# A three-stage kernel (clustered attention, dense MLP, mixture of experts): the order of work on ScalarE and GpSimd among the expert tiles, and of one subtraction at the start

## The chip, the cores and the metric

The kernel runs on one core of one Trainium2 chip. The metric is the device time of one execution in microseconds (us). Every time beyond the table of runs comes from one execution that the hardware profiler recorded. The engines are named as the profile names them: PE (TensorE's matmuls), PEld (its weight loads), DVE (VectorE), ACT (ScalarE), POOL (GpSimd) and SP (SyncE, which only starts DMAs here).

## What is computed

Three functions follow one another, all in float32:

```python
q_assign = argmax(q_n @ c_n.T)                 # nearest of 16 centroids, per head
mask = q_assign[..., :, None] == k_assign[..., None, :]
scores = where(mask, scale * q @ k.T, -1e9)
attn = softmax(scores) @ v                     # 2 batches, 8 heads, 768 tokens, 64
x = attn.reshape(1536, 512)
h = x @ w_in
x = (h * sigmoid(h)) @ w_out                   # 512 -> 2048 -> 512
logits = x @ w_gate + modality_bias[modality_id]
e_idx = argmax(logits)                         # 8 experts
gate_w = softmax(logits)[e_idx]
out = gate_w * (relu(x @ w1[e_idx]) @ w2[e_idx])   # 512 -> 1024 -> 512
```

## The kernel before

Products in float32 are made of three matmuls each: every operand is split into a high part (a copy rounded for PE) and a low part (the operand minus its high part). The helper at L200 subtracts, those at L202 and L209 copy (on ACT, and on POOL or DVE). So every weight and every activation is converted by two instructions on two engines before PE can use it.

**Attention** works through eight head pairs. For a pair, the loads of q, k and v come in on SP; q is scaled (L404, POOL, for every pair but the first); q and k are transposed (L422 is one of the ways, on DVE), split into high and low parts (for the low part of the first pair's k: two subtractions L200 on POOL, into `opn_0KX`) and moved to other partitions by DMAs on SP (L489). The cluster of each token is found by `c0` to `c5` (L503 to L523: transposes and reductions on DVE, one matmul L519 on PE). PE then does scores (L594 and L597), transposes of the probabilities (L633) and the product with v (L699). The reciprocals of the sums go to a buffer in memory (L686, `rsc<-rr`) and come back spread over partitions (L691, `rb<-rsc`) for the scaling on DVE at L704. At the start PE runs matmuls on a constant (L304) whose results nobody reads.

**The dense MLP** lies between 231 and about 520 us; the change doesn't touch its code.

**The experts.** After the routing the tokens of each expert stand in rows of an index table. Twelve tiles of 128 tokens (0 to 11) follow one another, and four small slots for what is left over (`SMALL_AT` names the tiles behind which they stand; `small` is the function). For one tile `slot` issues:

- the gather of its rows from `x2d` by an indirect DMA on POOL (L1403), each row with 512 numbers and, behind them, its 8 gate logits;
- four transposes on PE (L1408), the copy to high on ACT (L1412) and the low part on DVE (L1415);
- the first product, 24 matmuls (L1429), into two banks of 512;
- for each of the two banks the ReLU on ACT (L1444), four transposes on PE (L1449), a copy on ACT (L1454) and a subtraction on DVE (L1457);
- the second product, 24 matmuls (L1471);
- the exponential of the gate logits with its sum on ACT (L1481), three short operations on DVE (L1484 to L1488) that make 1/sum;
- the output scaling on ACT (L1495) and the scatter to the output, an indirect DMA on POOL (L1498).

A small slot has the same steps with 64 or 32 rows (gather L1537, first product L1560, ReLU L1567, transposes L1572, copy L1576, second product L1589, exponential L1596, output L1606, scatter L1609). The weights of an expert come in eight chunks on SP (L1360 and L1363; a load is skipped at run time where the next tile has the same expert), and each chunk is split by L202 on ACT and L200 on DVE.

**What sets the order.** The instructions of each engine stand in a fixed order in the program. It is found when the kernel is built: every piece of work is given to `op` with an estimated duration, the pieces that it depends on, the buffers it uses and a priority, and `Sched.run` plays the engines forward, taking on each engine the ready piece with the smallest `prio`. The tables `cp` (tiles) and `cs` (small slots) hold offsets to the priorities of the kinds of pieces (`tx` for the gathered rows' transposes and, before, the exponential; `rl` for the ReLU; `ga` for gathers), and `gl` and `late` are the planner's figures for how long a gather takes. A dependency in these lists shapes the order only; on the chip an instruction waits for the data and buffers that it uses. An engine does its instructions strictly in order, so one that waits holds all behind it.

The exponential of a tile was placed by these two calls:

```python
oe = op("Act", 1480 if t == 0 else 195, fe, deps=[og, M1[4]], uses=[gb, eb], alloc=[eb], prio=tx)
o = orel = op("Act", 480, fr, deps=[o_m, orel], uses=[hs_, hbs[x]], alloc=[] if x else [hs_], prio=pr + cp["rl"])
```

Of the kernel before, what the change touches and what calls it, by code (L numbers as in the profile page):

```python
# [228 lines left out]
def attention(tc, sc, pools, q, k, v, centroids, ident, xT, opts):  # L229
    nc = tc.nc  # L230
    if True:
# [14 lines left out]
        op = sc.op  # L246
# [45 lines left out]
        o = op("DVE", 400, cnorm1, deps=[o_cl], prio=-90)  # L292
        o = op("Act", 100, lambda: nc.scalar.activation(cn, css, AF.Sqrt), deps=[o], prio=-90)
        o = o_norm = op("DVE", 1900, cnorm2, deps=[o], prio=-90)
# [19 lines left out]
        o = op("PE", 213, ctr, deps=[o, o_id], uses=[mbc], alloc=[mbc], prio=-90)  # L314
# [20 lines left out]
        raws, ops, Sops, xops, wait, held = {}, {}, {}, {}, [], {}  # L335
# [39 lines left out]
        def prep(p):  # L375
# [156 lines left out]
            o = scores  # L532
            cl = []
            steps = [dve(c0), dve(c1), dve(c2), dve(c3), [("PE", 163, c4)], dve(c5)]
            for n, a in enumerate(steps):
                o = op(a, 0, None, deps=[o], uses=[cb] + ([mb] if n in (0, 4, 5) else []), alloc=[cb] if n == 0 else [],
                       prio=base + (5 + 0.1 * n if p else 0.1 * n), hold=not p, port=n == 2 and p > 0)
                cl.append(o)
            okops = []
# [39 lines left out]
        def chunk_ops(p, h, c, i, grp, both):  # L579
# [84 lines left out]
            if i % 3 == 2:  # L664
# [42 lines left out]
                r = op("SP", 1100, fW, deps=w["ops"], uses=[w["r"]], prio=pf("W"), xfer=opts["XW"], name=f"W{i}")  # L707
# [32 lines left out]
SMALL_AT = (2, 6, 8, 11)  # L740
# [10 lines left out]
def moe(tc, sc, pools, att, xT, w_in, w_out, mod_id, w_gate, mod_bias, w1, w2, out, ident, tails, opts):  # L751

    nc = tc.nc
    if True:
# [14 lines left out]
        def op(eng, dur, fn, prio=0.0, **kw):  # L769
            return sc.op(eng, dur, fn, prio=prio + 1000.0, **kw)  # L770
# [490 lines left out]
        cp = dict(w1=-57.1, w2=-33.6, ws=4.5, m1=-34.4, m2=-0.9, tx=-53.8, rl=-24.5, ga=-51.2, gg=15, gl=1500, late=500.0, kT=5, g0=15, g4=15, gx=14,  # L1261
# [105 lines left out]
        def slot(op, t):  # L1367
# [121 lines left out]
            oe = op("Act", 1480 if t == 0 else 195, fe, deps=[og, M1[4]], uses=[gb, eb], alloc=[eb], prio=tx)  # L1489
            oe = op("DVE", 160, fe2, deps=[oe], uses=[gb, eb], prio=tx, port=True)  # L1490
            oe = op("DVE", 80, fe3, deps=[oe], uses=[eb], prio=tx)
# [10 lines left out]
        def small_slot(s):  # L1502
# [74 lines left out]
            o = op("Act", 480, fr, deps=[o], uses=[hs_, hb], alloc=[hs_], prio=pr + cs["rl"])  # L1577
# [23 lines left out]
            oe = op("Act", 195, fe, deps=[og, M1[4]], uses=[gb, eb], alloc=[eb], prio=pr + cs["tx"])  # L1601
            oe = op("DVE", 240, fe2, deps=[oe], uses=[eb], prio=pr + cs["tx"])
# [11 lines left out]
        cs = dict(pr=11.3, w=-47.6, ga=-58.3, tx=-36.7, m1=-25.9, rl=-9.4, m2=10.7, late=2500.0, n1=1, n2=1)  # L1614
# [21 lines left out]
def routed_attention_kernel(tc, q, k, v, centroids, w_in, w_out, mod_id, w_gate, mod_bias, w1, w2, out):  # L1636
# [27 lines left out]
    warm2=24,  # L1664
    g1=1,
# [30 lines left out]
```

## Time and profile before

| | |
|---|---|
| median of 3 timed runs | 710.28 us (710.03 to 710.56) |
| the profiled execution's own time | 706.15 us |
| its span from first to last instruction | 704.2 us |
| busy PE / DVE / ACT / POOL | 688.8 / 507.4 / 417.3 / 122.4 us |
| largest wait of PE | 2.1 us, L1449 for ACT's L1444 |

The profile is of one execution, and a sum that is made from its durations is made against 706.15 us. In a row of the timeline the number in brackets is how long the engine had been idle before the instruction, and the arrow names what ended the idle time. A count (x4) stands where several instructions of a kind follow one another. "PEclk" is the share of full speed that TensorE's clock was granted in a stretch: 1.00 is 2.4 GHz, and 0.50 would be all of it at 1.2 GHz.

### The profile page before, as it was taken

The page shows a single profiled execution, that of the slowest core. Times are in us where ns is not written, and L with a number is a line of the kernel's source. Part 1 is how long each engine was busy: PE and PEld are TensorE (multiplying, and loading weights), DVE is VectorE, ACT ScalarE, POOL GpSimd, SP SyncE. Part 2 cuts the span into 40 slices and gives each one's busy share as a digit, 9 for nine tenths or more (in the row PEclk, how much of TensorE's full clock was granted, in tenths as well). Part 3 has the DMA queues.
Part 4 walks back from the last instruction along what each step waited for, and adds up shares of the span by engine and source line. Part 5 has one row for each costly group of instructions (what it writes and reads, how often), then busy time and mean ns, then how long its engine had stood idle before and what let it go on. Part 6 is the DMA issues. An engine that isn't in the chain of part 4 may idle for free.

```text
span 704.2 us, 11770 instructions
## 1 busy us (share of the span) xinstructions
PE 688.8 (98%) x4106; PEld 557.3 (79%) x4106; DVE 507.4 (72%) x977; ACT 417.3 (59%) x753; POOL 122.4 (17%) x158
## 2 busy tenths in 40 slices
PE   9999999999999999999999999999999989999994
PEld 7857777677686799999988999999878768787763
DVE  6878898897975789887478254432698978887830
ACT  5957778577676455554344243332646978896740
POOL 5422343242200000000003000000044123221011
PEclk9999999999999999999999999999999999999998
DMA  9965877752611676775105831000025487857750
GB/s 192 180 128 101 180 171 135 144 131 55 178 38 18 219 245 231 239 230 200 48 31 169 311 120 60 30 1 1 0 94 155 153 309 267 309 188 242 242 191 19
DMA packets 104338, 104.82 MB, mean 149 GB/s; under 512 B 70668, under 2 KB 75024, under 8 KB 104272
## 3 DMA queue, kind: packets, MB, share of 16 engines
q1 hardware_dynamic: 101728, 96.56, 47.7%
q0 software_dynamic: 2400, 7.41, 3.1%
q8 instruction: 34, 0.56, 0.4%
q14 instruction: 32, 0.26, 0.2%
q10 hardware_dynamic: 144, 0.03, 0.0%
HBM read 104.99 MB, written 15.17 MB: 171 GB/s over the span
## 4 chain that ended last, share of the span: by engine, by line
PE 87%; ACT 3%; DMA 3%; issue 2%; DVE 2%; POOL 0%; SPq 0%; POOLq 0%; DVEq 0%; ACTq 0%
PE bank L1302 19%; PE bank L1343 18%; PE bank L1429 9%; PE t L699 9%; PE bank L1471 7%; PE t L633 7%; PE big L594 5%; PE big L597 4%; ACT p L622 2%; PE bank L1449 1%; DMA row<-x2d,idin 1%; PE bank L1589 1%; PE bank L1560 1%; PE t L471 1%; PE t L304 1%
## 5 line engine op out<-in xcount | busy, mean ns | idle before, releaser
L1302 PE MATMUL bank<-whl,whl 128*128 128x384 f32 x768 | 145.7, 338 | 0.6 <-DVE whl L200 0.6
L1302 PEld LDWEIGHTS bank<-whl,whl 128*128 128x128 f32 x768 | 135.5, 188 | 6.4 <-DVE whl L200 1.0
L200 DVE TENSOR_TENSOR whl<-w,whl 128x1024 fp32r<-128x1024 f32 (+2 forms) x100 | 112.7, 1162 | 20.2 <-ACT whl L202 20.1
L622 ACT ACTIVATE p<-big,nm 128x768 f32<-128x768 f32 x96 | 86.8, 904 | 34.8 <-DVE nm L616 33.0
L616 DVE TENSOR_REDUCE nm<-big 128x1 f32<-128x768 f32 x96 | 89.9, 950 | 15.2 <-PE big L597 14.3
L202 ACT ACTIVATE whl<-w 128x1024 fp32r<-128x1024 f32 (+2 forms) x96 | 95.0, 1030 | 6.8 <-PE bank L1429 2.4
L633 PE MATMUL t<-ident,p 128*128 128x128 f32 x576 | 75.9, 273 | 1.0 <-DVE w L704 1.0
L633 PEld LDWEIGHTS t<-ident,p 128*128 128x128 f32 x576 | 66.7, 141 | 9.7 <-issue 5.6
L1471 PE MATMUL bank<-whl,w 128*128 128x512 f32 x288 | 74.2, 404 | 0.0
L1429 PE MATMUL bank<-whl,xb 128*128 128x512 f32 x288 | 71.9, 398 | 0.0
L202 ACT ACTIVATE pt<-t 128x384 f32<-128x384 f32 x129 | 58.2, 494 | 19.6 <-PE t L633 19.5
L699 PE MATMUL t<-pt,rawv 128*64 128x384 f32 x384 | 68.3, 494 | 0.0
L1429 PEld LDWEIGHTS bank<-whl,xb 128*128 128x128 f32 x288 | 52.6, 188 | 13.0 <-PE bank L1560 1.2
L1471 PEld LDWEIGHTS bank<-whl,w 128*128 128x128 f32 x288 | 52.9, 190 | 12.0 <-issue 0.8
L1079 POOL TENSOR_SCALAR row<-L,mx 128x8 f32<-128x8 f32 x12 | 4.6, 384 | 268.4 <-PE bank L1046 143.0
L699 PEld LDWEIGHTS t<-pt,rawv 128*64 128x64 f32 x384 | 25.0, 136 | 31.4 <-issue 31.2
L200 DVE TENSOR_TENSOR whl<-wraw,whl 128x1024 fp32r<-128x1024 f32 x31 | 37.9, 1223 | 14.1 <-ACT whl L202 14.0
L202 ACT ACTIVATE whl<-wraw 128x1024 fp32r<-128x1024 f32 x31 | 32.6, 1056 | 24.9 <-DVE wraw L940 21.8
L1343 PE MATMUL bank<-whl,g_0w 128*128 128x512 f32 x144 | 38.2, 392 | 0.0
L1343 PE MATMUL bank<-whl,g_2w 128*128 128x512 f32 x144 | 37.8, 394 | 0.0
L594 PE MATMUL big<-opn_0K,opn_0QQ 128*128 128x384 f32 x96 | 36.1, 380 | 1.2 <-ACT p L622 1.0
L1343 PE MATMUL bank<-whl,g_1w 128*128 128x512 f32 x144 | 37.2, 392 | 0.0
(301 smaller groups left out, 1095.7 us busy)
## 6 DMA issues: line engine op xcount, KB each, us to landing
w<-in_moe_w_dram SPq DMA_DIRECT2D x88, 512.0 KB
w<-in_moe_w_out_dram SPq DMA_DIRECT2D x8, 1024.0 KB
wraw<-wsc SPq DMA_DIRECT2D x16, 512.0 KB
wsc<-wraw SPq DMA_DIRECT2D x15, 512.0 KB
w<-in_moe_w_in_dram SPq DMA_DIRECT2D x7, 1024.0 KB
wraw<-in_moe_w_dram SPq DMA_DIRECT2D x8, 512.0 KB
x2d<-row SPq DMA_DIRECT2D x12, 260.0 KB
rawv<-in_v_dram SPq DMA_DIRECT2D x8, 384.0 KB
```

Source lines behind the costliest of these rows:

```text
L200: (nc.vector if e == "DVE" else nc.gpsimd).tensor_tensor(dst, a, b, op)
L202: nc.scalar.activation(dst, a, AF.Copy, scale=1.0 if scale is None else scale)
L594: nc.tensor.matmul(sb.tile[:, x, :HALF], t["QQ"][:, h, cs], t["K1"][:, h, sl(x)], start=True, stop=False)
L597: nc.tensor.matmul(sb.tile[:, x, :HALF], t["QX"][:96, h, cs], t["KX"][:96, h, sl(x)], start=False, stop=True)
L616: nc.vector.tensor_reduce(nb.tile, sb.tile[:, :, :HALF], AX.XY, ALU.max, negate=True)
L622: nc.scalar.activation(pb.tile.rearrange("p (a b) -> p a b", a=2), sb.tile[:, :, :HALF], AF.Exp, bias=nb.tile[:, 0:1], scale=1.0, accum_ou ...
L633: nc.tensor.transpose(tbs[x].tile[:, j * P:(j + 1) * P], pb.tile[:, kc * P:(kc + 1) * P], ident)
L699: nc.tensor.matmul(yb.tile[rows[z], :HALF], raws[p]["v"][0].tile[:, z, kc], w["grp"][z]["tile"][:, kc], start=(kc == 0), stop=(kc == NC6 - 1))
L1302: nc.tensor.matmul(hb.tile[:, :HALF], w[:, ws, dc, fs], xx[:, s, cs], start=(dc == 0 and n == 0), stop=(dc == 3 and n == 2))
L1343: nc.tensor.matmul(ab.tile, gb.tile[gs][:, js], w[:, ws, fc % 2], start=(fc == 0 and n == 0), stop=(fc == 15 and n == 2))
L1429: nc.tensor.matmul(hbs[x].tile, xs_[:, s, dc], w.tile[:, ws, x * 512:(x + 1) * 512], start=(dc == 0 and n == 0), stop=(dc == 3 and n == 2))
L1471: nc.tensor.matmul(ob.tile, hT.tile[:, s, fc * P:(fc + 1) * P], w.tile[:, ws, i * 512:(i + 1) * 512], start=(fc == 0 and n == 0), stop=(fc ...
```

## The change

Six edits, all to the planner's inputs; no instruction is added or taken away. The dependencies that are added (`cl[2]`, `orel`) don't add waits on the chip.

```diff
--- before.py
+++ after.py
@@ -536,6 +536,8 @@
                 o = op(a, 0, None, deps=[o], uses=[cb] + ([mb] if n in (0, 4, 5) else []), alloc=[cb] if n == 0 else [],
                        prio=base + (5 + 0.1 * n if p else 0.1 * n), hold=not p, port=n == 2 and p > 0)
                 cl.append(o)
+            if p == 0:
+                los["k", 1].deps.append(cl[2])
             okops = []
             for h in range(2 if p else 0):
                 okops.append(op([("Pool", 481, lambda h=h: c7(h)("Pool"))], 0, None,
@@ -704,7 +706,7 @@
                     nc.vector.tensor_tensor(xT[b][hp][:, col:col + HALF].rearrange("m (j p) -> m j p", j=3),
                                             yb.tile[:, :HALF].rearrange("m (j p) -> m j p", j=3),
                                             rb.tile.rearrange("m p j -> m j p"), ALU.mult)
-                r = op("SP", 1100, fW, deps=w["ops"], uses=[w["r"]], prio=pf("W"), xfer=opts["XW"], name=f"W{i}")
+                r = op("SP", 1100, fW, deps=w["ops"], uses=[w["r"]], prio=pf("W"), xfer=opts["XW"], late=opts["WL"] * (p == 0), name=f"W{i}")
                 r = op("SP", 1200, fB, deps=[r], uses=[rb], alloc=[rb], prio=pf("B"), xfer=opts["XB"], name=f"B{i}")
                 pts = [w["grp"][z]["buf"] for z in range(2)]
                 last, parts = None, opts["PARTS"]
@@ -737,7 +739,7 @@
 NBASE = 12
 NSM = 4
 NXS = 2
-SMALL_AT = (2, 6, 8, 11)
+SMALL_AT = (3, 6, 8, 11)
 NFIRST = 2
 NSLOT = NTC + NE + 1
 NCOL = NSLOT + NSM
@@ -1258,7 +1260,7 @@
                 lambda: V.scalar_tensor_tensor(idsc[:, :NXS], idin[:, NSLOT:NSLOT + NXS], 4.0, padc[:, :NXS], ALU.mult, ALU.add),
                 lambda: V.scalar_tensor_tensor(idsc[:, NXS:], idin[:, NSLOT + NXS:NCOL], 2.0, padc[:, NXS:], ALU.mult, ALU.add)], uses=[is_])
 
-        cp = dict(w1=-57.1, w2=-33.6, ws=4.5, m1=-34.4, m2=-0.9, tx=-53.8, rl=-24.5, ga=-51.2, gg=15, gl=1500, late=500.0, kT=5, g0=15, g4=15, gx=14,
+        cp = dict(w1=-57.3, w2=-35.1, ws=4.9, m1=-28.2, m2=-3.0, tx=-51.8, rl=-32.9, ga=-54.4, gg=15, gl=740, late=1500.0, kT=5, fe=-4.0, g0=15, g4=15, gx=14,
                   hi='AAAAAAAA', lo='DDDDDDDD', xyh='DDAAAADD', xyl='DDDDDDDD')
         EN = {"A": "Act", "D": "DVE", "P": "Pool"}
         for b in range(2):
@@ -1486,9 +1488,9 @@
 
             def fe3(eb=eb):
                 V.reciprocal(eb.tile[1], eb.tile[1])
-            oe = op("Act", 1480 if t == 0 else 195, fe, deps=[og, M1[4]], uses=[gb, eb], alloc=[eb], prio=tx)
-            oe = op("DVE", 160, fe2, deps=[oe], uses=[gb, eb], prio=tx, port=True)
-            oe = op("DVE", 80, fe3, deps=[oe], uses=[eb], prio=tx)
+            oe = op("Act", 1480 if t == 0 else 195, fe, deps=[og, M1[4], orel], uses=[gb, eb], alloc=[eb], prio=pr + cp["fe"])
+            oe = op("DVE", 160, fe2, deps=[oe], uses=[gb, eb], prio=pr + cp["fe"], port=True)
+            oe = op("DVE", 80, fe3, deps=[oe], uses=[eb], prio=pr + cp["fe"])
 
             def fo(t=t, ob=ob, os_=os_, eb=eb):
                 os_.tile = sbt(os_, [P, 512])
@@ -1574,7 +1576,7 @@
             def fh():
                 hT.tile = sbt(hT, [P, 512])
                 nc.scalar.copy(hT.tile[:, :NF], tbs.tile[:, :NF])
-            o = op("Act", 480, fr, deps=[o], uses=[hs_, hb], alloc=[hs_], prio=pr + cs["rl"])
+            o = orel = op("Act", 480, fr, deps=[o], uses=[hs_, hb], alloc=[hs_], prio=pr + cs["rl"])
             o = op("PE", 430, fT, deps=[o], uses=[hs_, tbs], alloc=[tbs], prio=pr + cs["rl"])
             h = op("Act", 480, fh, deps=[o], uses=[hT, tbs], alloc=[hT], prio=pr + cs["rl"])
             o = None
@@ -1598,8 +1600,8 @@
             def fe2():
                 V.tensor_scalar(eb.tile[1], eb.tile[1], 1e-9, None, ALU.add)
                 V.reciprocal(eb.tile[1], eb.tile[1])
-            oe = op("Act", 195, fe, deps=[og, M1[4]], uses=[gb, eb], alloc=[eb], prio=pr + cs["tx"])
-            oe = op("DVE", 240, fe2, deps=[oe], uses=[eb], prio=pr + cs["tx"])
+            oe = op("Act", 195, fe, deps=[og, M1[4], orel], uses=[gb, eb], alloc=[eb], prio=pr + cs["fe"])
+            oe = op("DVE", 240, fe2, deps=[oe], uses=[eb], prio=pr + cs["fe"])
 
             def fo():
                 os_.tile = sbt(os_, [P, 256])
@@ -1611,7 +1613,7 @@
             o = op("Act", 350, fo, deps=[o, oe], uses=[ob, os_, eb], alloc=[os_], prio=pr)
             scat.append(op("Pool", 1040, fs, deps=[o] + scat[-1:], uses=[os_], prio=pr + 20, xfer=364, name=f"scatters{s}"))
         scat, smalls = [], []
-        cs = dict(pr=11.3, w=-47.6, ga=-58.3, tx=-36.7, m1=-25.9, rl=-9.4, m2=10.7, late=2500.0, n1=1, n2=1)
+        cs = dict(pr=13.7, w=-37.6, ga=-62.1, tx=-41.6, m1=-28.9, rl=1.3, m2=7.5, late=0.0, fe=-2.0, n1=1, n2=2)
         for t in range(NBASE):
             slot(op, t)
             for s in range(NSM):
@@ -1662,6 +1664,7 @@
     XW=1500.0,
     XB=500.0,
     warm2=24,
+    WL=750.0,
     g1=1,
 )
```

`cl[2]` is step `c2` of the clusters (L511, DVE); `los["k", 1]` is the second subtraction of the first pair's k. `late` adds time to the planner's estimate of when a DMA's data have come.

What follows is how the instructions stand in the programs. Line numbers of the changed kernel are 2 higher from L537 on (L1481 is L1483, and so on). The numbers behind names only tell buffers apart.

First place: POOL in the first microseconds of attention; `opn_0KX` holds the low parts of the first pair's k, `rawq` the next pair's q, `lq` its low part. Before:

```order
L209 TENSOR_SCALAR opn_0K_256<-full_277 128x2x384
L200 TENSOR_TENSOR opn_0KX<-full_275,opn_0K_256 64x384
L200 TENSOR_TENSOR opn_0KX<-full_277,opn_0K_256 64x384
L404 TENSOR_SCALAR rawq_217<-rawq_217 128x768
L200 TENSOR_TENSOR lq_345<-full_319,opn_1QQ 128x384
L200 TENSOR_TENSOR lq_345<-full_339,opn_1QQ 128x384
```

and in the change:

```order
L209 TENSOR_SCALAR opn_0K_256<-full_277 128x2x384
L200 TENSOR_TENSOR opn_0KX<-full_275,opn_0K_256 64x384
L404 TENSOR_SCALAR rawq_217<-rawq_217 128x768
L200 TENSOR_TENSOR opn_0KX<-full_277,opn_0K_256 64x384
L200 TENSOR_TENSOR lq_347<-full_316,opn_1QQ 128x384
L200 TENSOR_TENSOR lq_347<-full_335,opn_1QQ 128x384
```

L404 moved from behind the second of the first pair's subtractions to between the two.

Second place: ACT among the expert tiles, at the two ReLU halves of tile 4 (L1444, now L1446; `wraw` is their result). `row_6380` is the gathered buffer of tile 6; the L202 ahead of the ReLU halves convert chunks 2 and 5 of tile 5's weights. Before:

```order
L202 ACTIVATE whl_6410<-w_2_4608 128x1024
L202 ACTIVATE whl_6420<-w_4_4628 128x1024
L1444 ACTIVATE wraw_6427<-bank_6322 128x512
L1481 ACTIVATE row_6380,gt_6435<-row_6380 128x8
L1444 ACTIVATE wraw_6427<-bank_6331 128x512
L202 ACTIVATE whl_6443<-w_7_4631 128x1024
L202 ACTIVATE whl_6451<-w_3_4613 128x1024
```

and in the change:

```order
L202 ACTIVATE whl_6393<-w_2_4608 128x1024
L202 ACTIVATE whl_6403<-w_4_4628 128x1024
L1446 ACTIVATE wraw_6411<-bank_6308 128x512
L1446 ACTIVATE wraw_6411<-bank_6316 128x512
L202 ACTIVATE whl_6423<-w_7_4631 128x1024
L202 ACTIVATE whl_6431<-w_3_4613 128x1024
L1456 CAST w_1_6444<-bank_6433 128x512
```

L1481 of tile 6 left the place between the two halves. Tile 6's exponential now stands 36 rows behind the second of them, behind tile 6's own ReLU halves.

Third place: POOL among the expert tiles; L1403 are the gathers of tiles, L1537 those of small slots, L1498 and L1609 the scatters of tiles and of small slots. The first row is tile 4's gather in both. Before (the gathers of tiles 4, 5, 6 and 7 are `row_6057`, `row_6148`, `row_6380`, `row_6556`):

```order
L1403 DMA row_6057<-x2d,idin 128x520
L1403 DMA row_6148<-x2d,idin 128x520
L1498 DMA out_dram<-row_6142,gt_5708 1536x512
L1537 DMA row_6265<-x2d,idin 128x520
L1498 DMA out_dram<-row_6340,gt_5997 1536x512
L1403 DMA row_6380<-x2d,idin 128x520
L1609 DMA out_dram<-row_6533,idsc 6144x128
L1403 DMA row_6556<-x2d,idin 128x520
```

and in the change (tiles 4, 5, 6 and 7: `row_6057`, `row_6136`, `row_6328`, `row_6477`; the scatters are those of tiles 1 and 2):

```order
L1405 DMA row_6057<-x2d,idin 128x520
L1500 DMA out_dram<-row_6091,gt_5816 1536x512
L1405 DMA row_6136<-x2d,idin 128x520
L1539 DMA row_6244<-x2d,idin 128x520
L1405 DMA row_6328<-x2d,idin 128x520
L1500 DMA out_dram<-row_6388,gt_6144 1536x512
L1405 DMA row_6477<-x2d,idin 128x520
```

Tile 6's gather moved from behind the scatter of tile 2 to ahead of it; tile 5's gather went behind tile 1's scatter.

## Rows read from the trace of the kernel before

**Rows 1.** The page's first part: busy time of each engine, share of the span, instructions.
```profile
PE 688.8 (98%) x4106; PEld 557.3 (79%) x4106; DVE 507.4 (72%) x977; ACT 417.3 (59%) x753; POOL 122.4 (17%) x158
```

**Rows 2.** Waits of PE: what waited for what; us in total, times, longest.
```profile
PE bank L1449 <- ACT wraw L1444: 2.1, 1, 2.1
PE t L633 <- DVE w L704: 1.0, 1, 1.0
```

**Rows 3.** Timeline around the experts' stall: start us, duration us, engine, line, operation, [idle before].
```profile
550.24 1.54 POOL L1498 DMA_INDIRECT out_dram<-row,gt  x1 [7.99 <-ACT row L1495]
...
563.90 0.33 SPq L1360 DMA_DIRECT2D w<-in_moe_w_dram  x1
...
570.47 2.01 ACT L202 ACTIVATE whl<-w 128x1024 fp32r<-128x1024 f32 x2 [1.04 <-DMA w<-in_moe_w_dram]
...
572.39 0.58 ACT L1444 ACTIVATE wraw<-bank 128x512 f32<-128x512 f32 x1
...
573.79 0.60 PE L1449 MATMUL bank<-ident,wraw 128*128 128x128 f32 x4
...
575.62 0.21 ACT L1481 ACTIVATE row<-row 128x8 f32<-128x8 f32 x1 [2.65 <-DMA row<-x2d,idin]
...
575.83 0.58 ACT L1444 ACTIVATE wraw<-bank 128x512 f32<-128x512 f32 x1
...
576.46 0.66 PE L1449 MATMUL bank<-ident,wraw 128*128 128x128 f32 x4 [2.07 <-ACT wraw L1444]
```

**Rows 4.** The chain that ended last, in order of time: start us, us, what.
```profile
562.44 0.44 PE bank L1449 x4
...
566.95 8.59 DMA row<-x2d,idin
...
576.46 0.66 PE bank L1449 x4
...
577.11 2.41 PE bank L1471 x6
...
579.52 2.41 PE bank L1589 x64
...
593.13 1.39 PE bank L1471 x6
...
634.80 1.88 PE bank L1589 x64
```

**Rows 5.** Windows: us, busy of PE PEld DVE ACT POOL, PEclk, DMA share, GB/s.
```profile
552.00:563.00 11.00, 11.00 (x63) 8.13 (x63) 10.93 (x15) 10.16 (x17) 1.41 (x1) 1.00 0.61 196
574.40:576.46 2.06, 0.00 (x1) 0.01 (x1) 0.54 (x1) 0.84 (x4) 0.00 (x0) 1.00 0.89 321
576.46:579.50 3.04, 3.04 (x14) 2.06 (x18) 1.23 (x1) 3.04 (x4) 0.00 (x0) 0.62 0.86 324
579.50:582.00 2.50, 2.50 (x66) 2.22 (x66) 0.93 (x2) 2.50 (x5) 0.00 (x0) 0.78 0.66 227
```

**Rows 6.** Timeline of attention's start and of two later operations like those.
```profile
9.65 1.00 POOL L200 TENSOR_TENSOR opn_0KX<-full,opn_0K 64x384 fp32r<-64x384 f32 x1
...
10.90 1.13 DVE L511 TENSOR_TENSOR clu_0e<-clu_0s,clu_0m 128x384 bf16<-128x384 f32 x1
...
11.59 1.13 POOL L404 TENSOR_SCALAR rawq<-rawq 128x768 f32<-128x768 f32 x1
...
11.87 0.55 SPq L489 DMA_DIRECT2D opn_0K<-opn_0K  x1
...
12.70 0.32 PE L519 MATMUL t<-clu_0t,tri 128*128 128x384 bf16 x1 [0.16 <-DVE clu_0t L515]
...
15.22 0.51 PE L597 MATMUL big<-opn_0KX,opn_0QX 96*128 96x384 f32 x2
...
27.66 0.56 DVE L511 TENSOR_TENSOR clu_0e<-clu_0s,clu_0m 128x384 bf16<-128x384 f32 x1
...
32.76 0.83 POOL L404 TENSOR_SCALAR rawq<-rawq 128x768 f32<-128x768 f32 x1
```

## The prediction

> **What bounds the kernel now.** I read the page first, for the share of TensorE (PE) and the chain that ends last; then the waits of PE; then the timeline, the chain in order of time and the granted clock around the one large wait. PE is busy for 688.8 us, 98% of the span [rows 1], so an engine beside PE counts only where PE waits for it. PE waits little: the largest wait is one of 2.1 us, at the transposes of an expert tile (L1449) for the ReLU before them (L1444); another that the change comes near is one of 1.0 us in attention, at L633 for L704 [rows 2].
>
> Where does that ReLU lose its time? The timeline tells it [rows 3]. ScalarE (ACT) does the first ReLU half of tile 4 at 572.39, and PE transposes it at 573.79. The second half could follow at 572.97, but ACT's next instruction in order is the exponential of tile **6** (L1481). Its input comes with that tile's gather, which POOL issued at 566.95 and which landed 8.59 us later, at 575.54 [rows 4]. ACT idled 2.65 us for it, did the exponential, and then the second ReLU at 575.83. PE resumed at 576.46 after 2.07 us without work [rows 3]. The exponential itself is needed only at tile 6's output, one and a half tiles on: a thing without hurry stood in front of one that PE was about to need.
>
> The stall has a second price. The granted clock is 1.00 in the stretches around, also in the idle 2.06 us; in the 3.04 us after it is 0.62, and in the next 2.50 us 0.78 [rows 5], so part of that time ran at the lower of the two levels, 1.2 instead of 2.4 GHz. The same work at the higher level shows what this cost [rows 4]: four transposes 0.66 against 0.44, six L1471 matmuls 2.41 against 1.39, sixty-four small L1589 matmuls 2.41 against 1.88. That is 0.22 + 1.02 + 0.53 = 1.77 us. The whole event costs 2.07 + 1.77 = **3.84 us**.
>
> **The change, part by part.** *The exponential behind its own tile's second ReLU.* Nothing is added or removed. Tile 6's exponential leaves the place between tile 4's ReLU halves and goes behind tile 6's own; the two halves of tile 4 now stand in a row on ACT (the second place in the section on the change). No wait for a gather is then left on ACT ahead of that ReLU: −3.84. What the exponential releases (two or three VectorE (DVE) operations on one column, then the output scaling) still comes a tile's second product ahead of its use, so moving it costs nothing.
>
> *The tables and the small slots.* They move tile 6's gather on POOL ahead of tile 2's scatter (third place), to the second place behind tile 1's, which stood at 550.24 [rows 3]: some 15 us earlier than 566.95. Even with the 8.59 us of this one it would then land before tile 4's ReLU. It is a second cure of the same stall, not a second gain. PE's instructions stay the same in number, so PE's busy time stays. But the margins move. Ahead of tile 4's ReLU halves on ACT stand, as before, two conversions (L202) of tile 5's weights, and the first waits for a load: ACT idled 1.04 us for it and began at 570.47; the load had been issued at 563.90 [rows 3]. With the exponential gone the halves would end at 572.97 and 573.55, against transposes at 573.79 and, one group of 0.44 later, 574.23: a margin of 0.7 to 0.8 us. PE comes earlier there, since small slot 0's two transposes (L1572) no longer stand ahead of it. Nothing in the trace shows the new wait. Its ends are 0, where the margin lasts, and 1.04, ACT's wait for the load; I take 0.25, near the lower end, because the rows leave a margin: +0.25.
>
> *The start.* POOL scales the second head pair's q (L404) between the two subtractions of the first pair instead of behind them (first place). In the rows [rows 6] DVE's L511 took 1.13 us while POOL subtracted, against 0.56 later, and PE's L519 came 0.16 us late at 12.70. Behind L519 PE works through its warm-up matmuls in order, so 0.16 is all that can be won. L404 takes 1.13 beside L511 and 0.83 alone: the subtraction that now comes third ends near 9.65 + 1.00 + 0.83 to 1.13 + 0.98 = 12.5 to 12.8 instead of 11.6; its result is first needed at 15.22. The key move behind it on SyncE (SP), at 11.87, goes to 12.8 to 13.1, and with it the v and q loads queued behind it; they have no reader for some us. If the late subtraction makes a DVE step wait instead of the early one, L519 comes up to 0.98, one subtraction, later. Ends −0.16 and +0.98; I take −0.10, near the end that the 0.16 sets, because L404 has one input and ends earlier: **−0.10**.
>
> The Trainium skill speaks against this part: "SBUF — State Buffer", section "SBUF: two separate sides", has VectorE and GpSimd hold their shared port pair as an exclusive lock for a whole instruction, VectorE's operations with two inputs included. By it L511 waits out whichever POOL operation came first, scaling or subtraction, this term is 0 instead of −0.10 and the time below 706.7 instead of 706.6; the trace's two long durations fit that reading too, and no row of before tells them apart.
>
> *The second move of the reciprocals of pair 0* (`late`) goes behind five more moves and loads of pair 2 on SP, at 0.55 each by the SP row at 11.87 some 2.8 us. Its reader is L704, and what PE does when that is late stands in the list of waits: 1.0 us at L633, for the first of the two moves [rows 2]. In the order nothing ahead of that first move changes, and only SP's order changes from this edit in attention. Ends −1.0 and +1.0, that wait gone or met a second time; I take 0.
>
> **Sum**: −3.84 + 0.25 − 0.10 = −3.69. The profiled execution took 706.15 us (span 704.2), so 702.46 profiled. The median of the timed runs is 710.28, 4.13 above it; I carry this over: 706.59, **706.6 us**. About 0.2%, 1.42 us either way, is what a measurement of this kernel can tell from no change.
>
> **The rivals.**
> 1. *The weight load takes the exponential's place.* Tile 5's load lands later than 570.4, since SP's order ahead of it also moved, and the two conversions hold the same ReLU. For it: ACT already waits 1.04 there. Against: the gather, which moved at the same time, is gone. To bring the event back whole it must land 2 us later than before; then −3.84 is returned and the time is 710.3 with the start. Chance 0.14.
> 2. *Slower: DVE is late for the first expert tiles.* From 552 to 563 DVE is busy 10.93 of 11.00 us [rows 5], and every low half of a weight chunk goes through it. The change runs tile 2's and tile 3's first product and the small slot's in another order there; a conversion that slips behind a newly placed one makes PE wait, and as the event above shows, a wait of some 2 us costs 3.84 with its clock [rows 3 to 5]. One such wait returns all that was won; it turns the sign when two tiles are hit in a row, tile 3 and tile 4: −3.84 + 2 × 3.84 = +3.84, 714.1. Against: PE was busy 11.00 of those 11.00 us all the same. Chance 0.15.
> 3. *Only the wait is won.* The timed runs may not have paid the 1.77 of the lower clock: −2.07 + 0.25 − 0.10 = −1.92, 708.4. Against: they lie within 0.53 us of each other, so a part of 1.77 that came and went would show. The Trainium skill ("TensorE: Matmul & The Clock Gate", section "What's actually happening") has the cold stretch differ from run to run of one kernel, which is this case; this trace, being one execution, shows neither. Chance 0.12.
> 4. *The start loses one subtraction*: +0.98 in place of −0.10: 707.7. Chance 0.07.
> 5. *The change does not do it*: the late gather holds something else. Against: it landed at 575.54, and tile 5's whole first product, which came after the L1589 matmuls of 579.52, stood between it and tile 6's transposes. 710.3, chance 0.02.
>
> **How the numbers follow.** The forecast has 0.50, with its own range from 705.3 (−3.84 − 0.16 − 1.0, every term at its lower end) to 707.9 (1.04 for the new wait, and half of the 1.0 of the reciprocals). Faster by over 0.2%: the forecast, 3 and 4: 0.50 + 0.12 + 0.07 = 0.69. Within 0.2%: 1 and 5: 0.16. Slower: 0.15. A range of 705.2 to 711.2 leaves out case 2 and little else: it reaches past 1 and 5 by the bounds of the unknown terms.
>
> **What would show it.** Right: no wait of L1449 for L1444 above 0.5 us; the exponential of tile 6 behind its ReLU; no slice near 576 under clock 1.00; PE's busy sum smaller by about 1.8, since slow matmuls count as busy; six L1471 matmuls at 1.39 throughout; the span near 700.5. The start's term: L519 at 12.55. Wrong: a wait at L1449 or at L1429 with ACT or DVE idle on a DMA before it (case 1), DVE full and PE waiting for `whl` from L200 between 540 and 560 (case 2), L511 still above 1 us (the start).

## The result, and the profile after

The changed kernel takes **701.32 us** (median of 4 runs, 699.55 to 703.41), the kernel before in the same comparison 710.15 us (4 runs, 709.96 to 710.56): 8.8 us less by the medians. The ratio that the comparison gave is 0.9852, with a 95% interval of 0.9819 to 0.9886; here and below the ratios are not quotients of the two medians (which would be 0.9876), and gains in us are differences of medians. The forecast was 706.6 and its range ended at 705.2: the direction came true, the size was more than twice the forecast. Of all runs below one, of e13_before_late_small, took 851.16 us at a mean granted clock of 0.752 and is left out of that kernel's median. The profiled execution of the changed kernel took 701.06 us, its span 699.2, against 706.15 and 704.2: 5.09 us less, where the sum gave 3.69.

The page's first part; the row to compare is [rows 1].

```profile
PE 684.9 (98%) x4106; PEld 555.6 (79%) x4106; DVE 506.8 (72%) x977; ACT 416.8 (60%) x753; POOL 126.5 (18%) x158
```

PE has the same 4106 instructions and is busy 3.9 us less. Of that, 1.5 us lie in the first 50 us, and other waits take them back: the first product of tile 2 starts at 540.87 us before and 540.92 after. What was won was won behind that point.

The waits of PE in the changed kernel (what waited for what: us in total, times, longest), against [rows 2], three of its lines:

```profile
PE t L635 <- DVE w L706: 1.4, 1, 1.4
...
PE bank L1591 <- ACT w L1578: 0.8, 1, 0.8
PE bank L1304 <- DVE whl L200: 0.6, 1, 0.6
```

The line for the ReLU (L1449 before, L1451 now) is gone. Among the experts PE waits once, 0.8 us at L1591 for the last small slot's copy, as it did before (0.82 at L1589); no tile makes it wait. Attention's wait at L635 is 1.4, where it was 1.0; in a second profile of the changed kernel (e5 below) it is 0.9.

The timeline at the former stall (start us, duration us, engine, line, operation, [idle before]), against [rows 3]:

```profile
569.52 1.28 ACT L1446 ACTIVATE wraw<-bank 128x512 f32<-128x512 f32 x2
...
570.00 2.90 PE L1473 MATMUL bank<-whl,w 128*128 128x512 f32 x12
...
572.64 1.06 ACT L202 ACTIVATE whl<-w 128x1024 fp32r<-128x1024 f32 x1 [0.90 <-DMA w<-in_moe_w_dram]
572.73 1.03 PE L1451 MATMUL bank<-ident,wraw 128*128 128x128 f32 x8
573.52 1.64 PE L1473 MATMUL bank<-whl,w 128*128 128x512 f32 x6
```

Tile 4's two ReLU halves run as one row of two on ACT and end at 570.80; PE comes for them at 572.73, 1.9 us later. ACT does wait for a weight load here, 0.90 us, but behind the ReLU. The exponential of tile 6 is far away, and its gather was issued early, as POOL's rows of the same timeline show:

```profile
548.24 1.93 POOL L1405 DMA_INDIRECT row<-x2d,idin  x1 [0.30 <-issue]
550.47 0.95 POOL L1539 DMA_INDIRECT row<-x2d,idin  x1 [0.30 <-issue]
551.73 1.51 POOL L1405 DMA_INDIRECT row<-x2d,idin  x1 [0.30 <-issue]
567.51 1.02 POOL L1500 DMA_INDIRECT out_dram<-row,gt  x1 [14.27 <-ACT row L1497]
...
600.12 0.21 ACT L1483 ACTIVATE row<-row 128x8 f32<-128x8 f32 x1
```

The row at 551.73 is tile 6's gather (566.95 before), the one at 600.12 its exponential, without any idle time ahead of it. The windows (columns as in [rows 5]) have the full clock throughout:

```profile
563.00:574.40 11.40, 11.40 (x58) 9.49 (x57) 9.72 (x15) 10.05 (x18) 2.19 (x2) 1.00 0.84 291
574.40:582.00 7.60, 7.60 (x38) 6.24 (x37) 7.60 (x12) 6.85 (x12) 0.77 (x1) 1.00 0.86 314
```

The start of attention, against [rows 6]:

```profile
9.13 1.00 POOL L200 TENSOR_TENSOR opn_0KX<-full,opn_0K 64x384 fp32r<-64x384 f32 x1
10.10 0.83 POOL L404 TENSOR_SCALAR rawq<-rawq 128x768 f32<-128x768 f32 x1
10.38 0.95 DVE L511 TENSOR_TENSOR clu_0e<-clu_0s,clu_0m 128x384 bf16<-128x384 f32 x1
10.90 1.29 POOL L200 TENSOR_TENSOR opn_0KX<-full,opn_0K 64x384 fp32r<-64x384 f32 x1
...
12.00 0.32 PE L519 MATMUL t<-clu_0t,tri 128*128 128x384 bf16 x1
```

L519 no longer waits (0.16 before), but L511 still takes 0.95, and POOL's second subtraction 1.29 where the first takes 1.00.

### The profile page after: what moved, and what is told of

The parts are those of the page before. It is cut to its first block, busy times and chain, and to the rows that moved or that the text cites. A ratio compares the mean times of both kernels' runs of the same rounds, so it can differ in the third digit from the quotient of the medians.

```text
span 699.2 us, 11768 instructions
## 1 busy us (share of the span) xinstructions
PE 684.9 (98%) x4106; PEld 555.6 (79%) x4106; DVE 506.8 (72%) x977; ACT 416.8 (60%) x753; POOL 126.5 (18%) x158
## 5 line engine op out<-in xcount | busy, mean ns | idle before, releaser
L200 DVE TENSOR_TENSOR whl<-w,whl 128x1024 fp32r<-128x1024 f32 (+2 forms) x100 | 112.6, 1165 | 7.1 <-ACT whl L202 6.4
L202 ACT ACTIVATE whl<-w 128x1024 fp32r<-128x1024 f32 (+2 forms) x96 | 94.6, 1027 | 8.9 <-DMA w<-in_moe_w_dram 3.1
L635 PE MATMUL t<-ident,p 128*128 128x128 f32 x576 | 75.9, 273 | 1.4 <-DVE w L706 1.4
L635 PEld LDWEIGHTS t<-ident,p 128*128 128x128 f32 x576 | 66.7, 141 | 10.1 <-issue 5.0
L1473 PE MATMUL bank<-whl,w 128*128 128x512 f32 x288 | 72.4, 398 | 0.0
L202 ACT ACTIVATE pt<-t 128x384 f32<-128x384 f32 x129 | 58.2, 493 | 20.1 <-PE t L635 20.0
L1473 PEld LDWEIGHTS bank<-whl,w 128*128 128x128 f32 x288 | 52.6, 188 | 11.5 <-issue 0.8
L200 DVE TENSOR_TENSOR whl<-wraw,whl 128x1024 fp32r<-128x1024 f32 x31 | 38.0, 1225 | 15.0 <-ACT whl L202 15.0
L202 ACT ACTIVATE whl<-wraw 128x1024 fp32r<-128x1024 f32 x31 | 32.7, 1057 | 25.7 <-DVE wraw L942 21.9
```

The costliest lines, as they stand in the source:

```text
L200: (nc.vector if e == "DVE" else nc.gpsimd).tensor_tensor(dst, a, b, op)
L202: nc.scalar.activation(dst, a, AF.Copy, scale=1.0 if scale is None else scale)
L635: nc.tensor.transpose(tbs[x].tile[:, j * P:(j + 1) * P], pb.tile[:, kc * P:(kc + 1) * P], ident)
L1473: nc.tensor.matmul(ob.tile, hT.tile[:, s, fc * P:(fc + 1) * P], w.tile[:, ws, i * 512:(i + 1) * 512], start=(fc == 0 and n == 0), stop=(fc ...
```

## The experiments

The theory after the result: the gather of tile 6 lands late, the exponential that reads it holds ACT, and with it PE; the changed kernel is free of this; and the kernel before pays more for it in most executions than in the one that was profiled. The rivals: the additional gain comes from other orders that the change makes (the small slots, attention), or from a fixed difference between profiled and timed runs.

**Is one profile of the kernel before like another?** e1_before_again and e5_after_again are the two kernels with no edit.

> The kernel before, unchanged, to see why its timed runs (710.15) lie 4 us above its profiled execution (706.15), which the changed kernel's do not (701.3 against 701.06). Theory A (the stall behind the exponential is larger or met a second time in most executions, because the gather lands later or another tile's gather is late too): most runs near 710, and a profile of such a run has a second wait of PE for ACT behind the exponential, or the same wait longer by 1 to 4 us with low clock after it. Theory B (a fixed cost outside the span): every span stays near 704 while the time is 710.

> The changed kernel, unchanged, beside the kernel before on one chip with many runs of both, since the kernel before ran from 704 to 712 us (median 708.0) in the last comparison and at 710 in the first. Theory A (the profiled 706.15 was an ordinary execution, and the 710 of the first runs the high end): the changed kernel at 701 to 702, 6 to 7 us under before. Theory B (the first comparison is the true one): 8 to 9 us under before.

Before: 707.81 us (12 runs, 705.11 to 711.0), ratio 1.0007 [0.9986, 1.0028]. After: 701.43 (6 runs, 700.88 to 702.2) against 707.1, ratio 0.9911 [0.9881, 0.9941], so 5.7 us faster. The kernel before is spread over several microseconds (22 runs of that comparison: 703.59 to 711.09), the changed one over 1.3. Theory B of e1 is out: in every run of before in the comparisons from here on, time less span is 1.7 to 2.1 us. Theory A's "most runs near 710" isn't met either, but its second wait is there. The waits of PE in this second profile of before:

```profile
PE big L597 <- DMA opn_1KX<-clu_0ok: 1.8, 1, 1.8
PE bank L1449 <- ACT wraw L1444: 1.8, 1, 1.8
PE bank L1429 <- DVE whl L200: 1.1, 1, 1.1
```

The first line lies in attention and goes up and down in both kernels (0.2 in the first profile of each, 1.1 in e15 of the changed kernel). The third line is a wait that the first profile doesn't have. Its timeline leads to the exponential of small slot 2 (L1596), which also waits for a gather:

```profile
598.61 0.21 ACT L1596 ACTIVATE row<-row 128x8 f32<-128x8 f32 x1 [2.58 <-DMA row<-x2d,idin]
598.94 0.16 DVE L1599 TENSOR_SCALAR gt<-gt 128x1 f32<-128x1 f32 x1 [2.97 <-ACT row L1596]
600.47 1.43 PE L1429 MATMUL bank<-whl,xb 128*128 128x512 f32 x5 [1.15 <-DVE whl L200]
```

ACT idles 2.58 us for the gather, DVE 2.97 for ACT, and DVE's weight conversions reach PE late. In the first profile the same exponential had waited 0.63 us and PE had felt nothing.

**One part of the change alone, or undone.** e2_exp_only puts the exponentials behind their own tile's ReLU and leaves the planner's numbers; e3_exp_undone is the changed kernel with the exponentials placed as before; e12_attn_only and e4_attn_undone do and undo the two edits in attention.

```diff
e2_exp_only (of before; the small slots likewise, with pr - 2.0)
-            oe = op("Act", 1480 if t == 0 else 195, fe, deps=[og, M1[4]], uses=[gb, eb], alloc=[eb], prio=tx)
+            oe = op("Act", 1480 if t == 0 else 195, fe, deps=[og, M1[4], orel], uses=[gb, eb], alloc=[eb], prio=pr - 4.0)
e3_exp_undone (of the changed kernel; the small slots likewise)
-            oe = op("Act", 1480 if t == 0 else 195, fe, deps=[og, M1[4], orel], uses=[gb, eb], alloc=[eb], prio=pr + cp["fe"])
+            oe = op("Act", 1480 if t == 0 else 195, fe, deps=[og, M1[4]], uses=[gb, eb], alloc=[eb], prio=tx)
e12_attn_only (of before)
+            if p == 0:
+                los["k", 1].deps.append(cl[2])
-                r = op("SP", 1100, fW, deps=w["ops"], uses=[w["r"]], prio=pf("W"), xfer=opts["XW"], name=f"W{i}")
+                r = op("SP", 1100, fW, deps=w["ops"], uses=[w["r"]], prio=pf("W"), xfer=opts["XW"], late=750.0 * (p == 0), name=f"W{i}")
e4_attn_undone (of the changed kernel)
-            if p == 0:
-                los["k", 1].deps.append(cl[2])
-    WL=750.0,
+    WL=0.0,
```

> The kernel before with only the exponentials (tiles and small slots) behind their own ReLU in the order; tables, small slots and attention as before. Theory A (the exponential in front of a ReLU is the whole cause): the largest waits of PE for L1444 are gone and the time is 701.3 to 703. Theory C (the new tables and the place of small slot 0 bring as much as the exponential): about half is won, 705 to 707.

> The changed kernel with the exponentials placed as before; the other edits stay. Tile 6's gather then stands behind tile 2's scatter again and its exponential ahead of tile 4's two ReLU halves. Theory A: the stall is back, 2 us or more of wait at L1451 for L1446 and a lower clock after it, 706 to 711. Theory C: most of the gain stays, 702 to 705.

> The kernel before with the two edits in attention alone (POOL's second subtraction of the first pair behind the scaling of q, and late for the reciprocals of pair 0). My term: 0.10 less than before, which runs of this spread cannot tell from nothing: 706.5 to 708.5; in the profile L519 waits less than 0.16 and L511 takes 0.95 to 1.13.

> The changed kernel without the two edits in attention (POOL's second subtraction of the first pair, late of the reciprocals). Theory A: 701.0 to 701.8, no difference that can be told, with L519 waiting 0.16 again. Theory D (the start is worth more than its 0.16, by a chain that follows): 702 to 703. If the wait of L635 for L706, 1.4 us in the changed kernel and 1.0 before, comes from these edits, it returns to 1.0.

e2: 704.64 us (12 runs) against 708.0, ratio 0.9958 [0.994, 0.9976], so 3.4 us, between the two theories' ranges: the tile 6 stall is gone, but with the old numbers the new order makes another wait, 28 us earlier:

```profile
547.08 1.05 ACT L202 ACTIVATE whl<-w 128x1024 fp32r<-128x1024 f32 x1
548.03 0.59 ACT L1444 ACTIVATE wraw<-bank 128x512 f32<-128x512 f32 x1
...
548.67 0.66 PE L1449 MATMUL bank<-ident,wraw 128*128 128x128 f32 x4 [1.29 <-ACT wraw L1444]
```

Here it is ACT's own work, a weight conversion in front of the ReLU, that PE waits for: so the planner's new numbers do carry a part of the gain.

e3: seven of nine runs between 702.81 and 705.57, about Theory C's range, two at 713.22 and 713.31, above Theory A's range, with a mean granted clock of 0.990 and 0.992 against 0.996 to 0.998 in the seven; the ratio 0.9982 [0.994, 1.0023] says nothing, the median (703.31) lies 4.7 under before's. In its profile tile 6's gather stands behind tile 2's scatter again, as before, and its exponential ahead of both ReLU halves:

```profile
564.02 1.43 POOL L1500 DMA_INDIRECT out_dram<-row,gt  x1 [12.16 <-ACT row L1497]
565.76 1.93 POOL L1405 DMA_INDIRECT row<-x2d,idin  x1 [0.30 <-PE bank L1410]
...
571.60 0.21 ACT L1483 ACTIVATE row<-row 128x8 f32<-128x8 f32 x1 [0.86 <-DMA row<-x2d,idin]
```

But the exponential starts 5.84 us after the gather's issue, where it was 8.67 in the first profile of before (566.95 to 575.62), and PE's waits for that ReLU come to 0.6 us. So with the new tables and neither of the two cures most executions escape the stall, with little margin. Why the gather lands sooner there was not tested (the gather's own row on POOL is 1.93 us long, and 3.52 in the four profiles of before with no edit). What the two long runs met was not in the profile.

e12: 707.95 (12 runs) against 707.1, ratio 1.0003 [0.9981, 1.0026]. e4: 701.68 (6 runs) against 708.0, 0.992 [0.9899, 0.9942], as the whole change. The attention edits are worth nothing that can be measured.

**The dependence on the gather taken away.** In these three variants of before the exponential keeps its place on ACT but reads a constant tile instead of the gathered logits (so the gate weights are not computed from the logits there): for all tiles from 2 on and the small slots (e6), for tile 6 alone (e7), for the small slots alone (e8).

```diff
-                nc.scalar.activation(gb.tile[:, DM:], gb.tile[:, DM:], AF.Exp, accum_out=eb.tile[1])
+                if t == 6:
+                    nc.scalar.activation(tmpb[:, 0], io8, AF.Exp, accum_out=eb.tile[1])
+                else:
+                    nc.scalar.activation(gb.tile[:, DM:], gb.tile[:, DM:], AF.Exp, accum_out=eb.tile[1])
```

(That is e7; e6 has `t >= 2` there and the constant in every small slot, e8 the small slots alone.)

> The kernel before in its own order, where the exponentials of tiles 2 to 11 and of the small slots read a constant of 8 columns instead of the gathered logits, so that they wait for no gather; the gate weights of those tokens are left out by this. Theory A (the cost is the wait for the gather in front of work that PE needs): 702 to 704.5, and a narrower spread than before's 704 to 712. Theory E (the spread and the rest come from elsewhere, from weight loads or the start): 706 or more with the same spread.

> As the last, for tile 6's exponential alone (its gate weights are left out). Theory A with my price of 3.84 (2.07 of wait and 1.77 of clock): 704.2 against 708.0. If the clock mostly stays up, as in the repeat's profile: 705.5 to 706.2, about 2 us.

> As the last, for the four small slots' exponentials alone (their gate weights are left out). The repeat's profile shows ACT held 2.58 us by small slot 1's, PE losing 1.15; the first profile shows 0.63 and no loss. Theory A: a gain of 0.5 to 1.5 us, 706.5 to 707.5. If small slots never matter: 708.0 as before.

Against 707.1: e6 702.48, ratio 0.9938 [0.9912, 0.9963]; e7 702.24, 0.9935 [0.9908, 0.9961]; e8 704.95, 0.9966 [0.9946, 0.9987]. The small slot meant in the expectation of e8 is number 2, counting from 0. By the medians tile 6's one exponential costs 4.9 us, where the profile had 3.84, and the small slots' cost 2.2, where it had none; both are more than expected. The two don't add up to more in e6 (4.6); the intervals are too wide to say how far they overlap. In e7's profile the exponential stands in its old place and nothing waits:

```profile
571.45 0.21 ACT L1482 ACTIVATE tmpb<-io 128x8 f32<-128x8 f32 x1
...
573.54 1.03 PE L1449 MATMUL bank<-ident,wraw 128*128 128x128 f32 x8
```

**The gather alone moved.** e11_gather6_first is before with two of POOL's rows exchanged, tile 6's gather and tile 2's scatter; every other engine keeps its order.

```diff
-                    prio=pr + cp["ga"], xfer=cp["gl"], late=cp["late"], name=f"gather{t}")
+                    prio=pr + cp["ga"] - 20 * (t == 6), xfer=cp["gl"], late=cp["late"], name=f"gather{t}")
```

> The kernel before with two rows swapped on POOL and nothing else: tile 6's gather ahead of tile 2's scatter instead of behind it. Its exponential stays between tile 4's two ReLU halves. Theory A (the wait for the gather is the cost, the exponential's place by itself none): the stall at L1449 is gone and the time is 702 to 704, as with the constant for tile 6's exponential (702.24). Theory F (the exponential's place is what counts, since the gather lands late in the burst anyway): 706 or more.

701.9 us (6 runs, 701.44 to 703.96) against 707.1, ratio 0.992 [0.9891, 0.995]: 5.2 us, where the whole change won 5.7 in e5's comparison. The exponential still stands between the halves, with its input long there:

```profile
571.45 0.59 ACT L1444 ACTIVATE wraw<-bank 128x512 f32<-128x512 f32 x1
...
571.92 0.22 ACT L1481 ACTIVATE row<-row 128x8 f32<-128x8 f32 x1
...
572.11 0.61 ACT L1444 ACTIVATE wraw<-bank 128x512 f32<-128x512 f32 x1
```

**The gather made later.** Five operations on a scratch tile on POOL stand ahead of the gather of tile 6 (e9 on before, e10 on the changed kernel), of small slot 2 (e13 on before), or of both (e14 on before, e15 on the changed kernel).

```diff
+                for _ in range(5 * (t == 6)):
+                    nc.gpsimd.tensor_scalar(tmpb, tmpb, 1.0, 1.0, ALU.mult, ALU.mult)
```

(In e13 `s == 2`, in the small slot's gather; in e14 and e15 both.)

> The kernel before with five short POOL operations (about 2 us by the 0.4 of others like them) ahead of tile 6's gather, on a buffer that nothing reads later. Theory A (before's time follows the landing of this one gather): 2 us or more longer than before, 709 to 711.5 against 707 to 708, and a wait of 3 to 5 us at L1449 with a lower clock after it. Theory E (the gather's landing is set by the burst of weight loads, whenever it is issued): within 1 us of before.

> The changed kernel with the same five operations ahead of tile 6's gather. Theory A: no difference, 700.9 to 702.2, since nothing that PE is about to need stands behind that gather any more.

> The kernel before with five short POOL operations ahead of small slot 2's gather (the one whose exponential held ACT 2.58 us in the repeat's profile), and tile 6's gather as before. They took 3.9 us ahead of tile 6's. Theory A2 (the same stall has a second place there, hidden in the first profile by luck): 2 to 4 us longer than before, 709 to 711, with a wait of PE for weights from L200 or for the small slot near 595 to 602. Rival: that place has slack and only tile 6's counts: within 1 us of before.

> Both gathers late, tile 6's and small slot 2's. Theory A2: 710 to 713, so the 710 of the first comparison is within reach of two such events in one execution. Rival: as with tile 6's alone, 708 to 709.

> The changed kernel with the same two gathers late. Theory A2: 700.5 to 702.5 as without, since no exponential there stands ahead of work that PE is about to need. If small slot 2's gather still holds something: 703 or more.

The five operations took 3.94 us, more than I had meant. e9: 708.54 against 707.1, ratio 1.0023 [1.0002, 1.0044]. Its profile, in which line numbers are 2 higher, has the stall enlarged:

```profile
564.95 3.94 POOL L1404 TENSOR_SCALAR tmpb<-tmpb 128x96 f32<-128x96 f32 x5
569.30 1.59 POOL L1405 DMA_INDIRECT row<-x2d,idin  x1 [0.41 <-issue]
...
576.54 0.21 ACT L1483 ACTIVATE row<-row 128x8 f32<-128x8 f32 x1 [6.43 <-DMA row<-x2d,idin]
```

PE waited 4.7 us there, as expected; the median rose by 1.4 us, less than the 2 that Theory A asked for. e13: 714.82 against 710.92 (this comparison ran on another chip), 1.0044 [1.002, 1.0069]; small slot 2's exponential waited 5.47 us, and PE 3.6 at L1429 for L200. e14: 713.65, 1.0022 [0.9997, 1.0047]; 2.7 us more than before: its delays together cost no more than one of them. Both lie above the ranges expected, as before itself does in this comparison. The changed kernel doesn't notice: e10 700.67, 0.9913 [0.9878, 0.9948]; e15 702.14 against 710.92, 0.9846 [0.9821, 0.9871].

**What the long executions of before hold.** e16_before_third and e17_before_fourth have no edit.

> The kernel before once more, for a profile beside those with a wait of ACT of 4.2 us at 541 (before L1412, PE losing 1.8) in the two kernels with late gathers. Theory A3 (that wait belongs to the order of before wherever it runs at 709 to 714): an execution of 709 or more shows it, with the waits at L1449 and near 600. Rival (it came with the added POOL operations): it is absent at any time of the execution.

> As the last, a second profile of the unaltered kernel before on the same chip: Theory A3 has the wait at 541 in an execution of 709 or more, its rival in none.

Medians 710.06 and 710.05 against 709.37 (ratios 1.0009 [0.9987, 1.0031] and 1.0006 [0.9976, 1.0035]); the profiled executions took 711.8 and 710.66, so this time the profile is of a long one. The waits of PE in e16:

```profile
PE bank L1449 <- ACT wraw L1444: 2.3, 1, 2.3
PE bank L1429 <- ACT xb L1412: 1.8, 1, 1.8
```

and in e17:

```profile
PE bank L1429 <- ACT xb L1412: 1.8, 1, 1.8
PE bank L1449 <- ACT wraw L1444: 1.7, 1, 1.7
PE bank L1429 <- DVE whl L200: 1.2, 1, 1.2
```

So Theory A3's wait is there in both, without any added operation. Besides the known two there is thus a third stall, at the start of the experts. In e16's timeline:

```profile
541.88 0.59 ACT L1412 CAST xb<-bank 128x512 fp32r<-128x512 f32 x1 [4.22 <-remote]
...
542.52 2.97 PE L1429 MATMUL bank<-whl,xb 128*128 128x512 f32 x8 [1.77 <-ACT xb L1412]
```

ACT stands still for 4.22 us in front of a copy whose input PE had finished some 3 us earlier; the trace names no releaser. In e17, e13 and e14 it stands 4.26, 4.16 and 4.29 us: in all four profiles of before and its variants that come from the two later comparisons in which before takes 709 to 711 us, on two chips, and in none from those in which it takes 707 to 708, on two others. Nor is it in the first profile of before, of 706.15 us, though the timed runs beside it took 710. Where it is absent the same copy waits 0.77 to 1.50 us for PE. Whether it goes with the chip or with the execution no run separates. Of the changed kernel there are two profiles from comparisons in which before takes over 709 (the first one, and e15), and neither has the stall. There the copy stands behind three conversions in a row; why that or anything else in the change should prevent it stays open. Two windows of e16, the first behind this stall, the second behind that of tile 6:

```profile
542.50:548.00 5.50, 5.48 (x16) 4.06 (x17) 4.66 (x5) 5.50 (x8) 0.00 (x0) 0.69 0.48 140
579.90:585.00 5.10, 4.76 (x56) 3.76 (x60) 1.75 (x2) 5.10 (x8) 0.00 (x0) 0.67 0.81 288
```

Both stretches run at a lowered clock. By the first row, the third stall costs 1.77 us of waiting and, as an estimate, 5.50 × (1 − 0.69) = 1.7 us of clock, some 3.5 together: about what lies between a gain of 8.8 and one of 5.7. It doesn't always cost that: in e14 the granted clock from 542.5 to 556 is 1.00, so there it cost its wait of 1.8 us alone.

## Why the prediction came out as it did

- **The mechanism was right.** The ReLU's wait is gone, the exponential stands behind its own tile's ReLU, no slice near 576 is under clock 1.00, and the six L1473 that follow take 1.64 us, where the same view of before has 2.65. Taking the dependence away (e7), moving the gather alone (e11) and delaying it (e9) shift the time the way that the theory says, e9 by less than expected.
- **Its size was perhaps too small.** The event was put at 2.07 + 1.77 = 3.84 from one execution; e7 has it at 4.9 by the medians, but its interval (2.8 to 6.5 us of 707.1) holds 3.84.
- **The added wait (+0.25) didn't come.** The halves end 1.9 us ahead of PE, and the load's 0.90 us on ACT fall behind them.
- **The start (−0.10)** can't be told from nothing (e4, e12). L519's 0.16 is gone in the profile, and L635 waits 0.4 longer there, though not in e5. L511 ends at 11.33, 0.40 after L404, and POOL's next subtraction then takes 1.29: this fits operations of the two engines that go one after the other, as the Trainium skill has it ("SBUF — State Buffer", section "SBUF: two separate sides": an exclusive lock). By that rule the term was 0; the measured value, with its interval, doesn't differ from 0.
- **"It is a second cure of the same stall, not a second gain"**: right. By the medians the earlier gather alone (e11) is worth 5.2, the moved exponentials alone 3.4 (e2), the whole change 5.7. The prediction gave the gain to the weaker of the two cures. It was wrong that the tables move the gather: with the tables alone (e3) and with the moved exponentials alone (e2, issued at 569.45) it stays behind tile 2's scatter, so the two together move it. And e3, with neither cure, still has its median 4.7 under before's: in most executions the tables and the place of the small slots escape the stall by themselves, where the prediction had them cost 0.25.
- **The step that failed** is "The median of the timed runs is 710.28, 4.13 above it; I carry this over". The 4.13 was read as an overhead that both kernels have. It is not: time less span is 1.95 us in the profiled execution of before, 1.86 in that of after, and 1.7 to 2.1 in every later run of before, so longer times are longer spans. The spans of the first comparison's runs of before aren't known; that the remainder was longer spans there too is inferred. Such executions can hold larger or further stalls, which the profile didn't show: small slot 2's exponential (waiting 0.63 without harm there; 2.58 in e1), tile 6's at 2.3, the third one at 541. The changed kernel isn't touched by the first two (e15), and showed none of the third; its median lies 0.26 above its profiled execution instead of 4.13. Which of the three the timed runs of the first comparison held was not recorded; that the third was among them is inferred from e13, e14, e16 and e17, and the one profile beside those runs (706.15) doesn't have it. The miss of 706.59 − 701.32 = 5.27 is this 3.87, and 1.40 by which the profiled execution did better than the sum. Of the 1.40, 0.25 is the wait that didn't come. Landmarks of the two traces place the rest: from tile 2's first product to the last small slot's L1589 the gain is 4.62, 0.78 above the event's 3.84, of which small slot 0's L1560 (1.07 + 0.57 + 0.57 us in three pieces before, 1.86 in one row now) is 0.35; from the last scatter to the end of the span it is 0.43 (7.30 to 6.87). No run separates these.
- **The rivals.** 1 and 2 didn't happen: no expert tile waits. 4 is within what e4 and e12 can't tell from nothing, and 5 fell with the result. Rival 3, that the timed runs don't always pay for the clock, was half right and pointed the wrong way: after waits of PE of 1.7 to 2.4 us at this place the clock stayed at 1.00 in e1, e8 and e17 and fell in the first profile and in e16. The Trainium skill ("TensorE: Matmul & The Clock Gate", section "What's actually happening") has the number of cold matmuls at a kernel's start differ from run to run; these executions show as much of a pause in the middle. The mean granted clock of before's 22 runs in e5's comparison goes from 0.991 to 0.998, the changed kernel's six have 0.996 to 0.998: some timed runs of before do pay for the clock, and the waits vary too; the two aren't separated. That the first runs lay within 0.53 us of each other was taken as evidence of no variation; three runs were too few: later the same kernel ran from 703.6 to 715.4.
- **From comparison to comparison** the gain differs, 5.7 us where before takes 707.1 and 8.8 where it takes 710 to 711, while the changed kernel stays at 701 to 702. What varies is the kernel before.

## What to carry to other kernels

Look on each engine for instructions without hurry that wait for a DMA in front of hurried ones, and try to move the DMA as well as the instruction (here the DMA alone won 5.2 us, the instructions alone 3.4); a DMA that is met with 0.6 us to wait in one profile costs PE a microsecond in the next. Before carrying a gap between profiled and timed runs over to the changed kernel, compare it with time less span: what is beyond that is longer spans, of executions that may hold stalls which this profile doesn't show, and a second profile of the same kernel may find them.

## What the runs showed of the hardware

The granted clock after a pause of PE isn't told by the pause's length in these runs. Behind the stall of tile 6 it stayed at full speed after 2.4 us in e8 (window, columns as in [rows 5]):

```profile
578.00:583.00 5.00, 4.95 (x79) 4.03 (x80) 1.92 (x2) 5.00 (x7) 0.00 (x0) 1.00 0.88 319
```

and it fell after 2.07 us in the first profile [rows 5] and after 4.7 in e9:

```profile
577.40:583.00 5.60, 5.60 (x62) 4.46 (x66) 2.09 (x3) 5.57 (x8) 0.00 (x0) 0.56 0.34 112
```

There 0.56 is close to the lower of the two levels. An ACT copy stood still for over 4 us, with its input written as far as the profile shows and no releaser in the trace (4.16 to 4.29 in e13, e14, e16 and e17), in some comparisons and not in others; what held it wasn't found.
